# Gate of chunks 6 to 11 for two token blocks by seven half-depth products, with six weight decode steps at other places and the sums' lo parts on GpSimd

## The chip, the cores and the metric

The kernel runs on one core of a Trainium2 chip. The metric is the device time of one execution in microseconds. The profile's times are counted from the start of its span. PE is TensorE (matmul), PEld its weight loads, ACT is ScalarE, DVE is VectorE, POOL is GpSimd, SP is the engine whose queue issues most of the DMAs.

## What is computed

Attention over 2 batches of 8 heads (576 positions, depth 64, causal, with a bias from cumulative sums), and on its output x (1152 tokens of 512) two feed-forward layers:

```
xn = x / sqrt(mean(x*x) + 1e-6) * rms_g
g  = xn @ w_gate                    # 512 -> 1536
x  = (silu(g) * (xn @ w_val)) @ w_out
h  = x @ w_in                       # 512 -> 2048
out = (h * tanh(softplus(h))) @ w_out2
```

All of it is float32. The change is in the first layer's gate.

## The kernel before, in words

**Numbers.** A float32 matrix is held as two parts, hi (rounded to PE's format) and lo (what is left), and a product is three matmul passes: hi by hi, hi by lo, lo by hi (`PASS`). Weights arrive as 64-bit words and are decoded on the chip, 128x512 a unit. A unit's decode has these steps: `w_load` (L311 on, issue at L315) brings 512 KB into one of four buffers r0 to r3; `shift` (L326) and the Prelu of `w_a` (L337) on ACT prepare the lower and the upper word; `w_b` (L344) ORs them on DVE; `w_hi` (L351) casts the hi part on ACT; `w_c` (L360) subtracts on DVE for the lo part. One call of `w_tick` moves this line on by one unit, in the order of the list `seq`: it finishes unit n, ORs up to unit n+1 and prepares up to n+2, and issues each load whose buffer is free. If the place of the unit is not free yet (`free`), the tick does nothing.

**Order.** There is no planner in this part: the program text is the order of each engine's queue, and an engine works through its queue in order. Where a tick stands in the text decides what ACT and DVE have in front of the next operation that PE waits for.

**First layer.** The 1152 tokens are three blocks of 384 (0, 1, 2), the 1536 columns are 12 chunks f of 128. Unit 2f is the gate of chunk f, 2f+1 its value; they lie in a ring of eight places. `gate_val(b, f)` (matmuls at L672) makes both for one block, 24 matmuls into a bank pair of the pool psS (two such buffers); `silu` applies Silu on ACT and multiplies on DVE. Chunks are taken in pairs f, f+1 (f = 2, 4, 6, 8, 10). Block 0 is done by `gate_val`. For blocks 1 and 2 the gates are done by `gates` (L690, two calls of 24 matmuls, one Silu of 768 columns each), and the values by `vals`, a Strassen-like scheme over (two halves of depth) x (two chunks) x (two blocks): seven products of six matmuls (`product`, L714) in place of eight, in the order a, b, c, d, a, c, d, into four banks (three of psT, one of psX); three banks are used twice, and between the two uses ACT copies a to p (L775) and DVE adds b, c and d (`add`, L700).

**Sums.** Three of the seven products take sums of a pair's weights, which `s_pair` makes when the pair's second value unit is decoded: four DVE adds of 256 columns (L379), two hi casts on ACT (L382), two lo subtractions on DVE (L384). Until then the pair's decoded words stay in their r buffers, and no load can go there. The sums lie in places of the output weights' units 8 to 11. The sums of the inputs (`xt`) are made once, before the loop.

**The loop** (L1156 on) takes the pairs 4 to 10: for pairs above 4 two `plain` steps of block 0 (a `gate_val`, one or two ticks, a `silu`), two `gates` with a tick each, and `vals` with a tick behind its first d product (for pair 10 there two `h_split` instead, which split the first results for the output stage). Then comes the output stage `y_acc` (L817), which takes the four banks of psT and psX for block 0, and later the second layer (L841, L887).

Of the kernel before, what the change touches and what calls it, by code (L numbers as in the profile page):

```python
# [42 lines left out]
def tile_kernel(ctx: ExitStack, tc: tile.TileContext, kq, qq, v, s, w1, w2, rms_g, out):  # L43
# [145 lines left out]
    def gates(h, x, pools):  # L189
        co = slice(64 + 288 * x, 352 + 288 * x)  # L190
        t = []
        for y, (pool, tag) in enumerate(pools):
            t.append(pool.tile([128, 512], F32, tag=tag, name="gates"))
            nc.tensor.matmul(t[y][0:68, 0:288], sel[:, y, h], cC[0:48, 0, co], start=True, stop=True)
        nc.scalar.copy(out=KB[0][64:68, S * h + 288 * x:S * h + 288 * x + 288], in_=t[0][64:68, 0:288])

        for c, n, o in ((0, 288, 288 * x),) if h == 0 else (((0, 288, 704),), ((0, 224, 992), (224, 64, 640)))[x]:
            nc.scalar.copy(out=QB[0][64:68, o:o + n], in_=t[1][64:68, c:c + n])
# [26 lines left out]
    NI, NU1 = 2 * NF, 3 * NF  # L225
    NUW = NU1 + 2 * NF2

    VS = (2, 4, 6, 8, 10)
    FY = (10, 11) + tuple(range(10))

    def pair_units(j):

        return [2 * j, 2 * j + 1, 2 * j + 3, 2 * j + 2]

    seq = list(range(2 * NPRE)) + [NI] + pair_units(4) + pair_units(6) + [NI + 1, NI + 2]
    seq += pair_units(8) + [NI + 3, NI + 4] + pair_units(10) + [NI + n for n in (10, 11, 5, 6, 7, 8, 9)]
    seq += [NU1 + n for n in (0, 1, 2, 3, 4, 5, 6, 10, 12, 14, 7, 30, 31, 9, 11, 13, 8, 16, 18, 20, 22, 15, 24, 26, 17,
                              19, 28, 21, 23, 25, 27, 29)]
    wring = [sbt([128, 2, 512], F32R, f"ring{y}", f"wring{y}") for y in range(9)]
# [2 lines left out]
    def w14_unit(n):  # L242
        return w14[:, n // 3].rearrange("p (x a m) -> p x a m", x=3, a=2)[:, n % 3]
# [17 lines left out]
    def unit(n):  # L261

        if n < NI:
            return ring_unit(n % 8)
        if n < NU1:
            return w14_unit(n - NI)
        n -= NU1
        if n < 9:
            return ring_late((8, 3, 4, 5, 6, 7, 0, 1, 2)[n])
        if n < 15:  # L270
            return slot_unit((0, 11)[n % 2 == 0], (n - 9) // 2)
        if n < 27:
            return w14_unit((n - 5) % 12)
        return slot_unit((7, 5)[n // 3 - 9], n % 3)

    gv_done, y_done = set(), set()

    def free(n):

        if n < NI:  # L280
            return n < 8 or (NB - 1, n // 2 - 4) in gv_done
        if n < NU1:
            return len(gv_done) > 0 if n < NI + 8 else (NB - 1, 11 if n < NI + 10 else 9) in gv_done
        n -= NU1
        last = FY[-1]
        if n < 6 or n in (10, 12, 14):
            return (NB - 1, 9 if n == 1 else 11) in gv_done
        if n < 9:
            return (n - 6, 11) in y_done
        if n < 15:  # L290
            return (1, last) in y_done
        if n < 27:
            return (NB - 1, (n - 5) % 12) in y_done
        return ((NB - 1, 7) if n < 30 else (0, last)) in y_done
# [58 lines left out]
    def w_c(n, hi=True):  # L353
        if hi:
            w_hi(n)
        kept[n] = conv.pop(n)
        c = kept[n][:, :, 0].bitcast(F32)
        w = unit(seq[n])
        eng = nc.vector if mlp else nc.gpsimd
        eng.tensor_tensor(out=w[:, 1], in0=c, in1=w[:, 0].bitcast(F32), op=ALU.subtract)  # L360
        if val_of(seq[n]) is None:
            kept.pop(n)
        elif val_of(seq[n]):
            s_pair(seq[n] // 2 - 1, n)

    s_v = {}

    def s_area(f, a):

        return w14_unit(8 + 2 * (VS.index(f) % 2) + a).rearrange("p a m -> p (a m)")  # L370

    def s_pair(f, n):

        (l1, h1), (l2, h2) = ([r[:, :, x].bitcast(F32) for x in range(2)] for r in (kept.pop(n - 1), kept.pop(n)))
        lo, hi = slice(0, 256), slice(256, 512)
        for o, x, y, op in ((h2[:, hi], l2[:, lo], l2[:, hi], ALU.add), (h2[:, lo], l1[:, lo], l2[:, lo], ALU.subtract),
                            (h1[:, lo], h2[:, hi], l1[:, lo], ALU.subtract),
                            (h1[:, hi], l1[:, hi], h1[:, lo], ALU.subtract)):
            nc.vector.tensor_tensor(out=o, in0=x, in1=y, op=op)  # L379
        s_v[f] = h, l = [s_area(f, a) for a in range(2)]  # L380
        for o, x in ((512, h2), (0, h1)):
            nc.scalar.copy(out=h[:, o:o + 512], in_=x)  # L382
        for o, x in ((512, h2), (0, h1)):
            nc.vector.tensor_tensor(out=l[:, o:o + 512], in0=x, in1=h[:, o:o + 512].bitcast(F32), op=ALU.subtract)  # L384

    def val_of(n):

        f = n // 2
        return f % 2 if n < NI and n % 2 and f - f % 2 in VS[1:] else None

    def freed():

# [266 lines left out]
    def h_at(b, f, n=1):  # L659
        z, y = h_slot(b, f)  # L660
        return h_tile(z)[:, y] if n == 1 else h_tile(z)[:, y:y + n]
# [34 lines left out]
    def quarter(r, c, b):  # L696
        return xhl[r][:, 2 * c:2 * c + 2, TB * b:TB * b + TB]

    def add(o, x, y, op=ALU.add):
        nc.vector.tensor_tensor(out=o, in0=x, in1=y, op=op)  # L700
# [5 lines left out]
    def split_pair(h, l, src):  # L706
        nc.scalar.copy(out=h, in_=src)  # L707
        nc.vector.tensor_tensor(out=l, in0=src, in1=h.bitcast(F32), op=ALU.subtract)  # L708
# [41 lines left out]
    def val_restored():  # L750

        c = h_tile("w0")[:, 4:7].rearrange("p a n -> p (a n)")
        for x in range(2):
            w = unit(2 * (VS[0] + x) + 1).bitcast(F32)
            add(c[:, 512 * x:512 * x + 512], w[:, 0], w[:, 1])
        a11, a12, a21, a22 = (c[:, 256 * n:256 * n + 256] for n in range(4))
        for o, x, y, op in ((a22, a21, a22, ALU.add), (a21, a11, a21, ALU.subtract),
                            (a11, a22, a11, ALU.subtract), (a12, a12, a11, ALU.subtract)):
            add(o, x, y, op)
        s_v[VS[0]] = h, l = [s_area(VS[0], a) for a in range(2)]  # L760
        split_pair(h, l, c[:, 0:1024])

    def vals(f, gaps):


        w1_, w2_ = unit(2 * f + 1), unit(2 * f + 3)
        s2, s4, s3, s1 = ([t[:, 256 * n:256 * n + 256] for t in s_v[f]] for n in range(4))
        a11, a12, a22 = ([w[:, a, o:o + 256] for a in range(2)] for w, o in ((w1_, 0), (w1_, 256), (w2_, 256)))
        x = {(c, b): (quarter(0, c, b), quarter(1, c, b)) for c, b in ((0, 1), (1, 1), (1, 2))}
        h11, h12, h21, h22 = h_at(1, f), h_at(1, f + 1), h_at(2, f), h_at(2, f + 1)  # L770
        p, q = h_tile("w6")[:, 6], h_tile("w6")[:, 7]
        a, b, c = (psT.tile([128, 512], F32, tag="T", name=n)[:, 0:TB] for n in ("pa", "pb", "pc"))
        d = psX.tile([128, 512], F32, tag="X", name="pd")[:, 0:TB]
        product(a, a11, x[0, 1], True)
        nc.scalar.copy(out=p, in_=a)  # L775
        gaps[0]()
        product(b, s2, xt[2], True)
        add(p, p, b)
        product(c, s3, xt[3], True)
        add(q, p, c)  # L780
        product(d, s1, xt[1], True)
        add(q, q, d)
        gaps[1]()
        product(a, a12, x[1, 1], False)
        add(h22, h22, q, ALU.mult)
        add(h11, h11, a, ALU.mult)
        product(c, a22, xt[4], False)
        add(q, p, c)
        add(h12, h12, q, ALU.mult)
        product(d, s4, x[1, 2], False)  # L790
        add(p, p, d)
        add(h21, h21, p, ALU.mult)
        for z in (1, 2):
            gv_done.update(((z, f), (z, f + 1)))

    def h_split(b, f):
        h = h_at(b, f)
        h_t[b, f] = hhl = sbt([128, 2, TB], F32R, ("hA", "hB", "mm")[(NF * b + FY.index(f)) % 3], "hhl")
        nc.scalar.copy(out=hhl[:, 0], in_=h)  # L799
        nc.vector.tensor_tensor(out=hhl[:, 1], in0=h, in1=hhl[:, 0].bitcast(F32), op=ALU.subtract)  # L800
# [339 lines left out]
    def ticks(n):  # L1140
        def run():
            for _ in range(n):
                w_tick()
        return run

    def plain(b, f, n):
        gate_val(b, f)
        ticks(n)()
        silu(b, f)
# [3 lines left out]
    plain(0, 4, 1)  # L1153
    vals(VS[0], (nothing, ticks(1)))
    plain(0, 5, 1)
    for f in VS[1:]:  # L1156
        if f > 4:
            plain(0, f, 1)
            plain(0, f + 1, 2)
        gates(1, f, ticks(1))  # L1160
        gates(2, f, ticks(1))
        vals(f, (nothing, ticks(1)) if f < VS[-1] else (nothing, lambda: [h_split(*s) for s in steps2[:2]]))
    h_split(*steps2[2])
    for k, (b, f) in enumerate(steps2):
        if k:
# [117 lines left out]
```

## Time and profile before

| What | Value |
|---|---|
| median of 3 runs | 535.59 us (534.05 to 539.03) |
| the profiled execution's own time | 534.76 us |
| its span | 532.7 us |
| PE busy | 521.3 us, 2948 matmuls |
| DVE busy | 352.7 us |
| ACT busy | 309.9 us |
| POOL busy | 58.9 us, 72 instructions |

The profile is of one execution; the rows further down are from it. Neighbouring instructions of an engine overlap, so the step from one start to the next is a little shorter than the duration. POOL's last instruction in it starts at 112.84 us; the pairs 2 to 10 of the first layer lie between 150 and 262 us.

### The profile page before, as it was taken

The numbers are of one execution on the slowest core, as the hardware profiler recorded it, in microseconds if no ns is written. First come the engines' busy times: TensorE is split into PE (matmuls) and PEld (weight loads), VectorE is DVE, ScalarE is ACT, GpSimd is POOL, SyncE is SP. The second block draws the span as 40 slices with busy tenths as digits, with TensorE's granted clock in tenths as the row PEclk, the third lists the DMA queues.
The fourth block names the chain that finished last, engine by engine and source line by source line (L and its number), as shares of the span: only waits on it lengthen the run. The fifth ranks groups of instructions, "written<-read, shape, count | busy, mean of one in ns | idle before, by whom it ended". The sixth has DMA issues, their size and how long they took to land.

```text
span 532.7 us, 7987 instructions
## 1 busy us (share of the span) xinstructions
PE 521.3 (98%) x2948; PEld 471.6 (89%) x2948; DVE 352.7 (66%) x727; ACT 309.9 (58%) x664; POOL 58.9 (11%) x72
## 2 busy tenths in 40 slices
PE   7998999999999999999999999999999999999997
PEld 4776776689999999999999999999889999999885
DVE  7798999954878576675567666376578667653321
ACT  5687897876365565657378776586624433333211
POOL 6254666310000000000000000000000000000000
PEclk8699999999999999999999999999999999999999
DMA  9999797203013243535155635254101000000101
GB/s 222 264 194 279 208 249 173 81 19 140 1 41 119 78 144 136 157 119 159 40 159 162 180 96 156 80 158 140 60 0 49 11 1 0 2 0 1 59 1 59
DMA packets 18782, 55.90 MB, mean 105 GB/s; under 512 B 2348, under 2 KB 2604, under 8 KB 18716
## 3 DMA queue, kind: packets, MB, share of 16 engines
q1 hardware_dynamic: 13520, 42.04, 25.3%
q0 software_dynamic: 3712, 9.70, 8.9%
q10 hardware_dynamic: 1512, 3.66, 2.8%
q8 instruction: 23, 0.38, 0.3%
q14 instruction: 15, 0.12, 0.1%
HBM read 52.73 MB, written 2.66 MB: 104 GB/s over the span
## 4 chain that ended last, share of the span: by engine, by line
PE 91%; DVE 4%; ACT 2%; issue 1%; DMA 0%; ACTq 0%; DVEq 0%
PE o L887 12%; PE gv L672 12%; PE y L817 9%; PE gv L841 8%; PE gv L690 8%; PE gv L887 6%; PE pa L714 5%; PE pd L714 5%; PE pc L714 5%; PE gv L817 5%; PE xa L552 4%; PE tp L514 4%; PE pb L714 2%; PE sc L466 2%; PE sc L467 2%; ACT px L498 1%
## 5 line engine op out<-in xcount | busy, mean ns | idle before, releaser
L672 PE MATMUL gv<-xh,wring 128*128 128x384 f32 x256 | 67.1, 338 | 0.2 <-DVE h_w L681 0.2
L344 DVE SCALAR_TENSOR_TENSOR r<-r 128x512 int32<-128x512 int32 x68 | 47.5, 703 | 10.0 <-ACT r L337 7.1
L817 PE MATMUL y<-hhl,w 128*128 128x384 f32 x288 | 50.2, 334 | 0.0
L817 PEld LDWEIGHTS y<-hhl,w 128*128 128x128 f32 x288 | 49.9, 188 | 0.0
L672 PEld LDWEIGHTS gv<-xh,wring 128*128 128x128 f32 x256 | 46.4, 188 | 0.4 <-DVE h_w L681 0.3
L326 ACT ACTIVATE r<-r 128x512 int32<-128x512 uint8 x60 | 41.1, 686 | 7.1 <-DMA r<-in_w_dram 7.1
L498 ACT ACTIVATE px<-sc,cst 128x384 f32<-128x384 f32 (+2 forms) x80 | 41.2, 528 | 6.4 <-DVE cst L491 6.3
L672 PE MATMUL gv<-xl,wring 128*128 128x384 f32 x128 | 43.1, 336 | 0.0
L690 PE MATMUL gv<-xh,wring 128*128 128x384 f32 x160 | 41.6, 336 | 0.0
L491 DVE CUSTOM_DVE_ANT_0 sc<-sc,xtm 128x384 f32<-128x384 f32 (+4 forms) x72 | 34.6, 500 | 5.8 <-PE sc L467 3.0
L337 ACT ACTIVATE r<-r 128x512 f32<-128x512 f32 x57 | 38.3, 672 | 0.0
L514 PE MATMUL tp<-cst,px 128*128 128x128 f32 (+1 forms) x200 | 31.0, 286 | 2.1 <-DVE xl L631 1.4
L708 DVE TENSOR_TENSOR glb<-u,glb 128x768 fp32r<-128x768 f32 x20 | 19.1, 956 | 18.2 <-ACT glb L707 18.2
L514 PEld LDWEIGHTS tp<-cst,px 128*128 128x128 f32 (+1 forms) x200 | 24.1, 145 | 6.9 <-DVE xl L631 1.9
L552 PE MATMUL xa<-aw,px 128*64 128x320 f32 (+3 forms) x192 | 30.1, 380 | 0.0
L690 PEld LDWEIGHTS gv<-xh,wring 128*128 128x128 f32 x160 | 29.0, 188 | 0.0
L800 DVE TENSOR_TENSOR hhl<-h_w,hhl 128x384 fp32r<-128x384 f32 x30 | 16.6, 558 | 18.5 <-ACT hhl L799 18.5
L690 PE MATMUL gv<-xl,wring 128*128 128x384 f32 x80 | 26.9, 336 | 0.0
L887 PE MATMUL o<-wt,glb 128*128 128x512 f32 x108 | 26.9, 390 | 0.0
L887 PE MATMUL o<-w,glb 128*128 128x512 f32 x108 | 26.5, 390 | 0.0
L466 PE MATMUL sc<-w 128*128 128x384 f32 (+1 forms) x64 | 24.3, 390 | 1.6 <-POOL w L130 1.5
L817 PE MATMUL gv<-hhl,w 128*128 128x384 f32 x144 | 25.1, 334 | 0.0
(269 smaller groups left out, 1252.3 us busy)
## 6 DMA issues: line engine op xcount, KB each, us to landing
r<-in_w_dram SPq DMA_DIRECT2D x66, 512.0 KB, 4.0
w<-in_kq_dram POOLq DMA_DIRECT2D x7, 576.0 KB, 6.2
w<-in_qq_dram POOLq DMA_DIRECT2D x7, 576.0 KB, 6.9
out_dram<-osb SPq DMA_DIRECT2D x8, 256.0 KB, 2.1
px<-in_v_dram SPq DMA_DIRECT2D x5, 320.0 KB
r<-in_w_dram ACTq DMA_DIRECT2D x2, 512.0 KB, 4.5
px<-in_v_dram ACTq DMA_DIRECT2D x3, 320.0 KB
raw_hA<-in_kq_dram SPq DMA_DIRECT2D x3, 288.0 KB
```

The costliest lines, as they stand in the source:

```text
L326: nc.scalar.activation(out=low, in_=low.bitcast(U8)[:, :, 3], func=ACTF.Copy, scale=1 / 32, bias=-15.5 / 32)
L337: nc.scalar.activation(out=top, in_=top, func=ACTF.Prelu, scale=2.0 ** -112, alpha=-2.0 ** 32)
L344: nc.vector.scalar_tensor_tensor(out=low, in0=top, scalar=3, in1=low, op0=ALU.logical_shift_left, op1=ALU.bitwise_or)
L498: nc.scalar.activation(out=pv, in_=sv, func=ACTF.Exp, bias=sbias[:, c + x:c + x + 1], scale=-1.0, accum_out=ssum[:, sc:sc + 1])
L514: nc.tensor.transpose(t[0:rows, o - a:o - a + 128], P[pos[i] % 2][:, o:min(e, o + 128)], ident)
L552: nc.tensor.matmul(o, V[z][0:rows, c, ds], r, start=(c == 0), stop=(c == (1, 4)[part]))
L672: nc.tensor.matmul(t[:, g, 0:TB], w[:, a, 128 * c:128 * c + 128], xhl[r][:, c, TB * b:TB * b + TB], start=(n == 0), stop=(n == 11))
L690: nc.tensor.matmul(t[:, g, 0:TB], w[:, a, 128 * c:128 * c + 128], xhl[r][:, c, TB * b:TB * b + TB], start=(n == 0), stop=(n == 11))
L714: nc.tensor.matmul(t, A[a][:, 128 * c:128 * c + 128], B[r][:, c], start=(start and n == 0), stop=(n == 5), skip_group_check=True)
L817: nc.tensor.matmul(y_t[b][d], w[:, a, 128 * d:128 * d + 128], hhl[:, r], start=(f == FY[0] and y == 0), stop=(f == FY[-1] and y == 2))
L841: nc.tensor.matmul(t[:, x, 0:TB], w[:, a, 128 * c:128 * c + 128], xhl[r][:, c, TB * b:TB * b + TB], start=(n == 0), stop=(n == 11))
L887: nc.tensor.matmul(o_t[b][tt], gl[:, r, x, 128 * tt:128 * tt + 128], w[:, a], start=(g == 0 and x == 0 and y == 0), stop=(g == NG - 1 and ...
```

## The change

A new function `gate_set(f, beside)` computes the gates of the pair f for blocks 1 and 2 as `vals` computes the values: seven products in the order a, b, c, d, a, c, d, in the same four banks, with a copy on ACT, five adds on DVE and four Silus of 384 columns. It is used for the pairs 6, 8 and 10 (`GS`); the pairs 2 and 4 keep `gates`. Its weights' sums are made by `s_pair` from the two gate units, which are therefore kept as the value units are; they lie in the places of the output units 6 and 7. The order of units is changed so that each pair's units that are kept stand together. The ticks stand at other places: one within `gate_set` behind the first product, one in `vals` behind the first product and one behind the d product, one behind `vals`; one instead of two in the second `plain`. In pair 10 the tick behind d comes after the two `h_split`. The lo parts of all sums that `s_pair` makes (of values too) are subtracted on GpSimd.

```diff
-    VS = (2, 4, 6, 8, 10)
+    VS, GS = (2, 4, 6, 8, 10), (6, 8, 10)
...
-        return [2 * j, 2 * j + 1, 2 * j + 3, 2 * j + 2]
+        v, g = [2 * j + 1, 2 * j + 3], [2 * j, 2 * j + 2]
+        return v + g if j in GS else g[:1] + v + g[1:]
-    seq = list(range(2 * NPRE)) + [NI] + pair_units(4) + pair_units(6) + [NI + 1, NI + 2]
-    seq += pair_units(8) + [NI + 3, NI + 4] + pair_units(10) + [NI + n for n in (10, 11, 5, 6, 7, 8, 9)]
+    seq = list(range(2 * NPRE)) + [NI] + pair_units(4) + pair_units(6)
+    for j, n in ((8, 1), (10, 3)):
+        seq += [NI + n] + pair_units(j) + [NI + n + 1]
+    seq += [NI + n for n in (10, 11, 5, 6, 7, 8, 9)]
...
         if n < NI:
+            if val_of(n) and n % 2 == 0 and n // 2 - 1 > GS[0] and (1, n // 2 - 3) not in g_done:
+                return False
             return n < 8 or (NB - 1, n // 2 - 4) in gv_done
+        if n in (NI + 6, NI + 7):
+            return (1, GS[-1]) in g_done
...
-        s_v[f] = h, l = [s_area(f, a) for a in range(2)]
+        (s_v if val else s_g)[f] = h, l = [s_area(f, a, val) for a in range(2)]
         for o, x in ((512, h2), (0, h1)):
             nc.scalar.copy(out=h[:, o:o + 512], in_=x)
         for o, x in ((512, h2), (0, h1)):
-            nc.vector.tensor_tensor(out=l[:, o:o + 512], in0=x, in1=h[:, o:o + 512].bitcast(F32), op=ALU.subtract)
+            nc.gpsimd.tensor_tensor(out=l[:, o:o + 512], in0=x, in1=h[:, o:o + 512].bitcast(F32), op=ALU.subtract)
 
     def val_of(n):
         f = n // 2
-        return f % 2 if n < NI and n % 2 and f - f % 2 in VS[1:] else None
+        return f % 2 if n < NI and f - f % 2 in (VS[1:] if n % 2 else GS) else None
...
+    def gate_set(f, beside):
...
+        h11, h12, p, q = h_at(1, f), h_at(1, f + 1), h_at(2, f), h_at(2, f + 1)
+        a, b, c = (psT.tile([128, 512], F32, tag="T", name=n)[:, 0:TB] for n in ("ga", "gb", "gc"))
+        d = psX.tile([128, 512], F32, tag="X", name="gd")[:, 0:TB]
+        product(a, a11, x[0, 1], True)
+        nc.scalar.copy(out=p, in_=a)
+        beside()
+        product(b, s2, xt[2], True)
+        add(p, p, b)
+        product(c, s3, xt[3], True)
+        add(q, p, c)
+        product(d, s1, xt[1], True)
+        add(q, q, d)
+        nc.scalar.activation(out=q, in_=q, func=ACTF.Silu)
+        product(a, a12, x[1, 1], False)
+        nc.scalar.activation(out=h11, in_=a, func=ACTF.Silu)
+        product(c, a22, xt[4], False)
+        add(h12, p, c)
+        nc.scalar.activation(out=h12, in_=h12, func=ACTF.Silu)
+        product(d, s4, x[1, 2], False)
+        add(p, p, d)
+        nc.scalar.activation(out=p, in_=p, func=ACTF.Silu)
+        g_done.add((1, f))
...
+    def first():
+        h_split(*steps2[0])
+        h_split(*steps2[1])
+        w_tick()
+
     for f in VS[1:]:
+        last = f == VS[-1]
         if f > 4:
             plain(0, f, 1)
-            plain(0, f + 1, 2)
-        gates(1, f, ticks(1))
-        gates(2, f, ticks(1))
-        vals(f, (nothing, ticks(1)) if f < VS[-1] else (nothing, lambda: [h_split(*s) for s in steps2[:2]]))
+            plain(0, f + 1, 1 if f in GS else 2)
+        if f in GS:
+            gate_set(f, ticks(1))
+        else:
+            gates(1, f, ticks(1))
+            gates(2, f, ticks(1))
+        vals(f, (ticks(1) if f in GS else nothing, first if last else ticks(1)))
+        if f in GS and not last:
+            w_tick()
```

## Rows read from the trace of the kernel before

**Rows 1.** Busy us, share of the span and instructions by engine.
```profile
PE 521.3 (98%) x2948; PEld 471.6 (89%) x2948; DVE 352.7 (66%) x727; ACT 309.9 (58%) x664; POOL 58.9 (11%) x72
```

**Rows 2.** Busy time by stretch; last columns: granted clock, DMA share, GB/s.
```profile
50.00:100.00 50.00, 48.00 (x351) 34.92 (x349) 47.01 (x149) 44.07 (x147) 30.28 (x29) 1.00 0.77 199
...
150.00:200.00 50.00, 50.00 (x290) 50.00 (x289) 35.92 (x65) 28.31 (x48) 0.00 (x0) 1.00 0.30 93
200.00:250.00 50.00, 50.00 (x290) 50.00 (x289) 32.81 (x60) 30.25 (x52) 0.00 (x0) 1.00 0.44 139
250.00:300.00 50.00, 50.00 (x290) 50.00 (x290) 33.15 (x59) 35.16 (x67) 0.00 (x0) 1.00 0.45 132
```

**Rows 3.** The chain that ended last: start us, us, what (150 to 262 us).
```profile
158.71 4.16 PE gv L672 x24
...
222.35 8.32 PE gv L690 x48
230.67 1.04 PE pa L714 x6
...
236.95 1.07 PE pd L714 x6
...
262.00 24.96 PE y L817 x144
```

**Rows 4.** ACT's instructions in time order: start us, us, line, operation (pairs 6 and 8).
```profile
212.67 0.69 ACT L326 ACTIVATE r<-r 128x512 int32<-128x512 uint8 x1
213.24 0.67 ACT L337 ACTIVATE r<-r 128x512 f32<-128x512 f32 x1
213.80 0.66 ACT L326 ACTIVATE r<-r 128x512 int32<-128x512 uint8 x1
...
218.23 0.49 ACT L680 ACTIVATE h_w<-gv 128x384 f32<-128x384 f32 x1 [3.21 <-PE gv L672]
...
231.82 0.79 ACT L694 ACTIVATE h_w<-gv 128x768 f32<-128x768 f32 x1
232.51 0.46 ACT L775 COPY h_w<-pa 128x384 f32<-128x384 f32 x1
232.87 0.66 ACT L351 CAST wring<-r 128x512 fp32r<-128x512 f32 x1
```

**Rows 5.** DVE's instructions in time order (pair 6).
```profile
204.55 0.42 DVE L379 TENSOR_TENSOR r<-r 128x256 f32<-128x256 f32 x1
204.89 0.75 DVE L379 TENSOR_TENSOR r<-r,r 128x256 f32<-128x256 f32 x2
205.68 0.43 DVE L379 TENSOR_TENSOR r<-r 128x256 f32<-128x256 f32 x1
206.11 1.42 DVE L384 TENSOR_TENSOR w<-r,w 128x512 fp32r<-128x512 f32 x2
...
210.91 0.56 DVE L700 TENSOR_TENSOR h_w<-h_w,pd 128x384 f32<-128x384 f32 x1 [0.49 <-PE pd L714]
211.38 0.68 DVE L344 SCALAR_TENSOR_TENSOR r<-r 128x512 int32<-128x512 int32 x1
211.99 0.68 DVE L360 TENSOR_TENSOR wring<-r,wring 128x512 fp32r<-128x512 f32 x1
```

**Rows 6.** POOL by line and shape: count | busy us, mean ns | idle before.
```profile
L360 POOL TENSOR_TENSOR wring<-r,wring 128x512 fp32r<-128x512 f32 x8 | 10.4, 1298 | 21.0 <-ACT wring L351 15.1 <-issue 5.8
```

**Rows 7.** DVE's instructions in time order, 85 to 93 us.
```profile
85.96 0.73 DVE L491 CUSTOM_DVE_ANT_0 sc<-sc,xtm 128x512 f32<-128x512 f32 x1
...
87.46 1.71 DVE L344 SCALAR_TENSOR_TENSOR r<-r 128x512 int32<-128x512 int32 x1
```

**Rows 8.** POOL's instructions in time order, 85 to 93 us.
```profile
85.64 1.04 POOL L612 TENSOR_TENSOR w<-w,cst 128x512 f32<-128x512 f32 x1 [2.42 <-DVE cst L606]
...
87.11 1.50 POOL L136 TENSOR_TENSOR w<-raw_mm,w 64x576 fp32r<-64x576 f32 x1
```

**Rows 9.** Weight loads issued from 150 to 270 us: issue to landing.
```profile
DMA to landing us min/median/max: 3.5/3.6/4.6
```

More of the change, by code (lines that the diff above doesn't have):

```diff
@@ L274, in unit @@
         return slot_unit((7, 5)[n // 3 - 9], n % 3)
-    gv_done, y_done = set(), set()
+    gv_done, y_done, g_done = set(), set(), set()
     def free(n):
         if n < NI:
+            if val_of(n) and n % 2 == 0 and n // 2 - 1 > GS[0] and (1, n // 2 - 3) not in g_done:
+                return False
             return n < 8 or (NB - 1, n // 2 - 4) in gv_done
+        if n in (NI + 6, NI + 7):
+            return (1, GS[-1]) in g_done
         if n < NU1:
@@ L363, in w_c, with s_area, s_pair @@
         elif val_of(seq[n]):
[L364 to L372, printed above, removed]
+            s_pair(seq[n] // 2 - 1, n, seq[n] % 2)
+    s_v, s_g = {}, {}
+    def s_area(f, a, val=1):
+        return w14_unit(8 + 2 * (VS.index(f) % 2) + a if val else 6 + a).rearrange("p a m -> p (a m)")
+    def s_pair(f, n, val):
         (l1, h1), (l2, h2) = ([r[:, :, x].bitcast(F32) for x in range(2)] for r in (kept.pop(n - 1), kept.pop(n)))
@@ L761, in val_restored @@
         split_pair(h, l, c[:, 0:1024])
+    def gate_set(f, beside):
+        w1_, w2_ = unit(2 * f), unit(2 * f + 2)
+        s2, s4, s3, s1 = ([t[:, 256 * n:256 * n + 256] for t in s_g[f]] for n in range(4))
+        a11, a12, a22 = ([w[:, a, o:o + 256] for a in range(2)] for w, o in ((w1_, 0), (w1_, 256), (w2_, 256)))
+        x = {(c, b): (quarter(0, c, b), quarter(1, c, b)) for c, b in ((0, 1), (1, 1), (1, 2))}
+        h11, h12, p, q = h_at(1, f), h_at(1, f + 1), h_at(2, f), h_at(2, f + 1)
[20 more added lines that the diff above has]
+        g_done.add((1, f))
     def vals(f, gaps):
```

## The prediction

> **What bounds the kernel now.** I read the busy shares first, then the table by stretches, then the chain that ended last, and only then the queues of ScalarE (ACT) and VectorE (DVE) around one pair of chunks. The shares show a TensorE (PE) kernel with an idle GpSimd [rows 1]. The stretches show more: from 150 to 300 us PE is busy in all of every 50 us at clock 1.00, while DVE is busy in 33 to 36 and ACT in 28 to 35 of them [rows 2]. The chain is there one unbroken line of matmuls, in order of the code [rows 3]. So a matmul taken out between 150 and 300 us is won in full, and anything that makes PE wait there is lost in full. DVE and ACT have a third of their time free on average, but they work through their queues in order, so what decides is what stands in front of the one operation that PE waits for.
>
> **What is removed.** Gate chunks f, f+1 of blocks 1 and 2 now take 48 matmuls, 8.32 us; a product of six takes 1.04 us [rows 3]. Seven products take 7.28 us: 1.04 us less a pair, and three pairs (6, 8, 10) make **3.12 us**, 0.6%. The 48 matmuls wrote banks of their own and needed ACT only for one Silu pass at the end. The seven products go through four PSUM banks, three of them twice, and a bank's second product may start only when ACT or DVE has read the first: a's after the copy to p, c's after the second add, d's after the third. The same rule holds in the value set that follows, where today it costs nothing [rows 3].
>
> **What is added.** A pair's set adds a copy, five adds of 384 columns, and four activations of 384 columns in place of two of 768; its weights' sums add four DVE adds of 256 columns, two casts and two GpSimd subtractions; two DVE subtractions of 512 columns go from the value sums. On DVE that is 4 x 0.34 + 5 x 0.47 - 2 x 0.60 = 2.5 us more per pair by start-to-start times [rows 4, 5], of some 24 us, and about 2 us more on ACT. Both fit by the average. Where they stand is another matter.
>
> **Set of pair 6.** Time runs from the end of its first product a. ACT copies p (the next operation starts 0.36 later), and then comes the tick that the change puts right there: shift and top of gate chunk 9 (0.57 and 0.56), the hi cast of value chunk 9 (0.66) [rows 4]. DVE has done its two OR steps, waits for that cast, subtracts (0.60), makes the four sums of the value pair 8 (three starts 1.13 apart in all, and 0.34), and only then adds b to p (0.47) and c to p (0.55) [rows 5]. With about 0.03 for each change of engine: 0.03 + 0.36 + 0.57 + 0.56 + 0.66 + 0.03 + 0.60 + 1.47 + 0.47 + 0.55 + 0.03 = 5.3 us. PE wants bank c again after products b, c, d and a, 4 x 1.04 = 4.2 us. It waits **1.2 us**. Only time from rows at full length enters here, so I give it 1.0 to 1.4.
>
> **Set of pair 8.** Here a load is late as well. Time runs from the end of value set 6's first d product. DVE adds (0.47), subtracts for gate chunk 9 (0.60), makes two sums (0.77); ACT casts (0.66); GpSimd subtracts twice, at 1.30 each [rows 6], to 5.1 us. Only then are the two buffers free into which value chunks 10 and 11 are loaded; a load lands 3.5 to 4.6 us after its issue [rows 9], so at about 9.0 and 10.0. ACT prepares both (2 x 1.13, to 11.3), and behind them in its queue stand the Silu of gate (0,8) (0.49, to 11.8), the preparation of gate chunk 10, the hi cast, the Silu of (0,9) and the copy p. DVE goes on at 11.8 with the product for (0,8) (0.47) and two OR steps (1.2), waits for the cast until about 14.3, and has before the set's first two adds: two subtractions (1.2), the product for (0,9) (0.47), an OR step (0.6), four sums (1.47); then the adds (1.0). That ends at 19.1. PE has 3 products, 8.32 us of gates of block 0, one product and then the 4.2 us of cover: 16.6. It waits 2.5; without any delay of the loads beyond 3.5 us and with GpSimd undisturbed 1.8, with 4.6 us for both 2.9. I take **2.4 us**.
>
> **Set of pair 10** has the same late loads in front, but no sums in its tick: 1.47 less, **1.0 us** (0.4 to 1.5). **First output product:** in value set 10 DVE now has two splits (0.47, 0.55) and a tick (0.60, 0.60) between the third add (0.47) and the two products that free bank a (0.47, 0.55): 3.7 us against 3 products, 3.1 us of cover: **0.6 us** (0.3 to 0.8), which the ticks moved to the end cause.
>
> **What costs nothing.** The gate sums of pair 6 are made in value set 4 and used some 17 us later (two gates of 4.16 and the set's first products lie between), those of pairs 8 and 10 as far ahead: 3.5 us of casts and subtractions are hidden. The number of ticks until the output stage is the same, so the loads behind it stay as they were. The sums' area is that of output chunks 6 and 7, which are converted after the last set, before they are wanted. If that cover were gone, each would cost its cast and subtraction, 1.3 us a chunk [rows 4, 5].
>
> **GpSimd in place of DVE.** The two subtractions take 1.30 us each there, 0.69 on DVE [rows 5, 6], and they are not free of DVE: where a GpSimd operation on two SBUF inputs ran, a DVE step with two SBUF inputs took 1.71 us instead of 0.69 [rows 7, 8]; one with a PSUM input stayed at 0.73 [rows 7]. The set's adds read PSUM, so they pass; of the value set one product of two SBUF tiles meets the pair, about 1.2 us, between two idle gaps. The Trainium skill (GPSIMD Engine Reference, Engine selection) says to leave elementwise work on VectorE because GpSimd takes about twice as long on two inputs. The trace agrees on the ratio (1.9), but by the rule's choice the subtractions would stand on DVE ahead of the adds that PE waits for: some 1.4 us more at pairs 6 and 8, and the sum would come out about 3 us longer.
>
> **Sum.** 1.2 + 2.4 + 1.0 + 0.6 = 5.2 us of waits against 3.1 us of matmuls: **2.1 us longer**; with the low ends 3.5 - 3.1, 0.4 longer, with the high ends 6.6 - 3.1, 3.5 longer. The profiled execution took 534.76 us (span 532.7, the rest lies around it), the median of the runs shown is 535.59. From the middle of both, 535.2, I forecast **537.2 us**, in its own range 535.2 to 539.5. The waits of 1 to 2.5 us leave the clock alone, as from 50 to 100 us, where PE stood idle for 2.0 us and had 1.00 [rows 2].
>
> **Rivals.** *All is covered* (0.2): PE waits at none of the four places, the time falls by 3.1 us to 532.1. For it: DVE and ACT have 15 us and more of every 50 free [rows 2], and the same order of adds costs nothing in the value sets today [rows 3]. Against it: today no tick stands between the copy and the adds; in the changed set one does, with 3.2 us of DVE work.
>
> *GpSimd holds everything up* (0.15): its subtractions and DVE take turns, so that they last longer than the rows 6 say. A factor of 1.4 makes 1.8 us of 1.30; the loads come 1.0 us later, sets 8 and 10 wait 1.0 us more each, the copy p misses the second a product by another 0.3 in each, set 6 waits 0.3 more: about 3 us, 540.2 us. Below 1.5 us each it changes nothing that can be seen, from some 2.2 us on it makes the kernel slower by over 1%. For it: DVE's step of 1.71 us [rows 7]. Against it: all eight of this form have 1298 ns as their mean, with DVE busy beside them [rows 6]. The Trainium skill (SBUF — State Buffer, Who interferes with whom) says the port is locked for a whole instruction and the loser waits it out; the 1.71 us agree. By that rule alone the pair of subtractions would hold a two-input step for 2.6 us, which is inside this rival.
>
> *The sums come too late* (0.05): the set's second product waits for them. It would take more than 15 us of delay; a wait of 2 us a pair would make 539 us.
>
> **How the numbers follow.** Forecast 0.6, the rivals 0.2, 0.15 and 0.05. The range from 532.0 to 541.0 takes in the covered case and the GpSimd case. A measurement of this kernel (534.05 to 539.03 in three runs) tells about 1%, 5.4 us, from no change. Faster by over 1% would need 530.2, more than all that is removed: 0.03, for what the runs scatter. Slower by over 1% (541.0) is the far half of the GpSimd case and some of the sums': 0.09. Within 1%: 0.88.
>
> **What would show it.** In the profile after: 18 matmuls fewer; in the chain that ended last, PE waiting at the second c product of each set, released by DVE's add, for about 1.2, 2.4 and 1.0 us, and 0.6 before the first output product; GpSimd subtractions of 1.3 us, fourteen of them; ACT waiting for the loads of value chunks 10 and 11. If PE shows no idle time between 190 and 262 us, the covered case is right; if GpSimd's operations are near 2 us, the second rival is; if PE waits at a set's second product, the third.

## The result, and the profile after

The change makes the kernel **slower by 1.0%**: ratio 1.0097 to the kernel before, 95% interval 1.0069 to 1.0125. On 534.66 us, the median of before over 19 runs, that is 5.2 us, or 539.8 us; the forecast was 537.2, with a range from 532.0 to 541.0. The ratio leaves out three slow executions among the changed kernel's 19 (their median with these three is 541.61 us), and the profiled one, 545.65 us, is one of the three. Its attention, whose code is unchanged, ended 5.8 us later than in the trace before. So I compare one stretch from here on, from the first matmul of `gates` (pair 2) to the first of the second layer; the scatter of the attention's length lies ahead of it. Before it runs from 150.2 to 336.7 us, 186.5 us; after from 156.0 to 347.9 us, **191.9 us**. That is 5.4 us more and agrees with the ratio.

First the busy shares of the changed kernel, and the same table by stretches as [rows 2]:

```profile
PE 523.2 (96%) x2930; PEld 470.3 (86%) x2930; DVE 368.6 (68%) x746; ACT 315.9 (58%) x679; POOL 76.4 (14%) x86
```

```profile
150.00:200.00 50.00, 50.00 (x290) 50.00 (x289) 35.83 (x63) 28.79 (x48) 8.84 (x6) 1.00 0.21 65
200.00:250.00 50.00, 45.95 (x254) 45.32 (x253) 35.18 (x69) 30.96 (x57) 10.79 (x8) 0.97 0.32 115
250.00:300.00 50.00, 48.52 (x276) 47.56 (x275) 36.17 (x64) 36.04 (x69) 0.66 (x1) 1.00 0.51 158
...
235.00:240.00 5.00, 3.36 (x11) 3.36 (x12) 2.56 (x6) 3.62 (x7) 2.56 (x2) 0.70 0.16 29
240.00:245.00 5.00, 5.00 (x29) 5.00 (x29) 3.10 (x6) 2.04 (x4) 0.00 (x0) 0.96 0.45 180
```

There are 2930 matmuls, 18 fewer, and 14 more operations on GpSimd: the change does what it says. But PE, which was busy in all of each 50 us, now lacks 4.05 us between 200 and 250 and 1.48 between 250 and 300. And the clock, which had been 1.00, shows 0.97 in the second stretch; the drop lies between 235 and 245 us. Where PE waits is said by the table of waits (who waited for whom: us in total, times, longest):

```profile
PE gc L722 <- DVE h_w L708: 4.1, 2, 2.7
...
PE gc L722 <- DVE h_ring L708: 1.2, 1, 1.2
...
PE y L854 <- DVE h_w L708: 0.2, 1, 0.2
```

`gc` is the bank c of the sets, L708 is `add`: PE waits at the second c product of each of the three sets, and the table has no other wait in them. The set of pair 8 in PE's instructions in order of time (start us, us; between the lines stand further matmuls of the same product):

```profile
231.73 1.20 PE L722 MATMUL gd<-xt,w 128*128 128x384 f32 x6
232.77 0.34 PE L722 MATMUL ga<-xh,wring 128*128 128x384 f32 x1
...
236.64 0.44 PE L722 MATMUL gc<-xt_mm,wring 128*128 128x384 f32 x1 [2.67 <-DVE h_w L708]
238.45 0.52 PE L722 MATMUL gd<-xh,w 128*128 128x384 f32 x1
240.37 0.36 PE L722 MATMUL pa<-xh,wring 128*128 128x384 f32 x1
241.44 1.21 PE L722 MATMUL pb<-xt,w 128*128 128x384 f32 x6
```

From the second a to the second c it takes 3.87 us where 1.05 would do: a delay of 2.82. From there to `pa`, two products, it takes 3.73 us in place of the 2.21 that the other two sets need: another 1.5 us, in which the matmuls run at half the clock (0.50, the 1.2 GHz level, from 237 to 240 us). The same steps give 1.55 us for pair 6 (208.12 to 210.72) and 1.40 for pair 10 (260.23 to 262.68). The output stage's first products lose some 0.8 us: from the end of value set 10 to the second layer it takes 75.7 us, before 74.9.

How it comes to the 2.82 us is seen in ACT's and DVE's instructions in order of time, the queues that [rows 4, 5] show for the kernel before:

```profile
226.89 0.66 ACT L333 ACTIVATE r<-r 128x512 int32<-128x512 uint8 x1 [1.38 <-DMA r<-in_w_dram]
227.45 0.65 ACT L344 ACTIVATE r<-r 128x512 f32<-128x512 f32 x1
228.10 0.67 ACT L333 ACTIVATE r<-r 128x512 int32<-128x512 uint8 x1
228.67 0.64 ACT L344 ACTIVATE r<-r 128x512 f32<-128x512 f32 x1
229.21 0.48 ACT L688 ACTIVATE h_w<-gv 128x384 f32<-128x384 f32 x1
...
231.87 0.48 ACT L781 COPY h_w<-ga 128x384 f32<-128x384 f32 x1
```

```profile
229.72 0.56 DVE L689 TENSOR_TENSOR h_w<-h_w,gv 128x384 f32<-128x384 f32 x1 [3.48 <-ACT h_w L688]
...
233.31 0.68 DVE L367 TENSOR_TENSOR wring<-r,wring 128x512 fp32r<-128x512 f32 x1
233.92 0.42 DVE L387 TENSOR_TENSOR r<-r 128x256 f32<-128x256 f32 x1
234.25 0.75 DVE L387 TENSOR_TENSOR r<-r,r 128x256 f32<-128x256 f32 x2
235.04 0.43 DVE L387 TENSOR_TENSOR r<-r 128x256 f32<-128x256 f32 x1
235.38 0.55 DVE L708 TENSOR_TENSOR h_w<-h_w,gb 128x384 f32<-128x384 f32 x1
236.03 0.56 DVE L708 TENSOR_TENSOR h_w<-h_w,gc 128x384 f32<-128x384 f32 x1
```

The operation at the head of ACT's queue waits until 226.89 for the load of value chunk 10. The Silu of block 0 (L688), long ready, stands behind it and the three further steps that prepare the two units; DVE stands idle for 3.48 us for it. Then DVE works with only one gap of 0.15 us, but the four sums (L387) are ahead of the add of bank c.

A wait of ACT for a load is not new. In the kernel before, ACT waits as long in each of these pairs (1.79, 1.88 and 1.72 us; here pair 8), and PE waits nowhere:

```profile
225.30 0.67 ACT L326 ACTIVATE r<-r 128x512 int32<-128x512 uint8 x1 [1.88 <-DMA r<-in_w_dram]
```

There block 0's last Silu is done at 222.9, ahead of that wait, and the 8.3 us of `gates` give PE work meanwhile. So what stands behind the load should count, and not the wait alone; e2 and e8 test this.

### The profile page after: what moved, and what is told of

Its sections match the earlier page's. It is cut to its first block, busy times and chain, and to the rows that moved or that the text cites. A ratio compares the mean times of both kernels' runs of the same rounds, so it can differ in the third digit from the quotient of the medians.

```text
span 543.9 us, 8036 instructions
## 1 busy us (share of the span) xinstructions
PE 523.2 (96%) x2930; PEld 470.3 (86%) x2930; DVE 368.6 (68%) x746; ACT 315.9 (58%) x679; POOL 76.4 (14%) x86
## 4 chain that ended last, share of the span: by engine, by line
PE 60%; issue 17%; DVE 9%; ACT 6%; DMA 5%; POOL 2%; SPq 1%; POOLq 0%; ACTq 0%; DVEq 0%
PE o L924 12%; PE y L854 9%; PE gv L878 8%; PE gv L924 6%; PE gv L854 5%; DMA r<-in_w_dram 4%; PE xa L560 3%; PE pa L722 3%; PE pc L722 3%; PE pd L722 3%; PE tp L522 2%; POOL w L392 2%; DVE sc L499 2%; PE pb L722 2%; ACT px L506 1%
## 5 line engine op out<-in xcount | busy, mean ns | idle before, releaser
L680 PE MATMUL gv<-xh,wring 128*128 128x384 f32 x256 | 67.0, 338 | 0.2 <-DVE h_w L689 0.2
L351 DVE SCALAR_TENSOR_TENSOR r<-r 128x512 int32<-128x512 int32 x68 | 50.3, 748 | 4.5 <-ACT r L341 2.2
L680 PEld LDWEIGHTS gv<-xh,wring 128*128 128x128 f32 x256 | 46.4, 188 | 0.4 <-DVE h_w L689 0.3
L680 PE MATMUL gv<-xl,wring 128*128 128x384 f32 x128 | 43.0, 336 | 0.0
L522 PE MATMUL tp<-cst,px 128*128 128x128 f32 (+1 forms) x200 | 32.6, 293 | 6.2 <-DVE w L594 1.9
L392 POOL TENSOR_TENSOR w<-r,w 128x512 fp32r<-128x512 f32 x14 | 20.3, 1470 | 110.5 <-ACT w L390 93.2
L367 DVE TENSOR_TENSOR w<-r,w 128x512 fp32r<-128x512 f32 x24 | 16.4, 689 | 13.0 <-ACT w L358 12.4
L854 PEld LDWEIGHTS gv<-hhl,w 128*128 128x128 f32 x144 | 25.0, 188 | 0.0
```

Source lines behind the costliest of these rows:

```text
L351: nc.vector.scalar_tensor_tensor(out=low, in0=top, scalar=3, in1=low, op0=ALU.logical_shift_left, op1=ALU.bitwise_or)
L522: nc.tensor.transpose(t[0:rows, o - a:o - a + 128], P[pos[i] % 2][:, o:min(e, o + 128)], ident)
L680: nc.tensor.matmul(t[:, g, 0:TB], w[:, a, 128 * c:128 * c + 128], xhl[r][:, c, TB * b:TB * b + TB], start=(n == 0), stop=(n == 11))
L854: nc.tensor.matmul(y_t[b][d], w[:, a, 128 * d:128 * d + 128], hhl[:, r], start=(f == FY[0] and y == 0), stop=(f == FY[-1] and y == 2))
```

## The experiments

All ratios are to the kernel before, measured together with it on the same chip. The stretch is the one defined above, from one profile of each kernel; it is the difference of the two columns as shown, so its last digit can be off by 0.1. The two kernels in which PE waits nowhere in this stretch and does the same work, before and e7, differ by 0.3 us.

| Kernel | First gate product, us | Second layer, us | Stretch | Ratio (95%) |
|---|---|---|---|---|
| before | 150.2 | 336.7 | 186.5 | |
| after | 156.0 | 347.9 | 191.9 | 1.0097 (1.0069 to 1.0125) |
| e1, sums later | 151.7 | 340.8 | 189.1 | 1.0039 (1.0007 to 1.0072) |
| e2, prepared later | 151.2 | 339.2 | 188.0 | 1.0018 (0.9988 to 1.0048) |
| e3, lo parts on DVE | 151.3 | 349.0 | 197.7 | 1.0227 (1.0166 to 1.0287) |
| e4, fill | 154.6 | 346.4 | 191.8 | 1.0131 (1.0071 to 1.0191) |
| e5, three repairs | 151.0 | 336.1 | 185.1 | 0.9960 (0.9927 to 0.9992) |
| e6, gates as before | 154.1 | 345.2 | 191.1 | 1.0092 (1.0061 to 1.0123) |
| e7, GpSimd alone | 149.2 | 336.0 | 186.8 | 1.0000 (0.9968 to 1.0032) |
| e8, e6 prepared later | 147.7 | 335.6 | 187.9 | 1.0010 (0.9979 to 1.0041) |
| e9, e5 with DVE | 149.4 | 336.1 | 186.7 | 1.0003 (0.9971 to 1.0036) |

**e1, the value sums behind the second a product.** In `w_c` a pair's sums are put aside while the set's tick runs; no load may take their buffers meanwhile.

```diff
+            if hold:
+                pend.append((seq[n] // 2 - 1, n, seq[n] % 2))
+            else:
+                s_pair(seq[n] // 2 - 1, n, seq[n] % 2)
...
         nc.scalar.activation(out=h11, in_=a, func=ACTF.Silu)
+        sums_now()
         product(c, a22, xt[4], False)
```

> The tick inside the set no longer makes the value sums at once: their four adds, casts and GpSimd subtractions stand behind the second a product. Theory (DVE's queue in front of the set's adds is what PE waits for): the wait before the second c product, 1.55 / 2.82 / 1.40 us in the sets of pairs 6 / 8 / 10 of the profile after, becomes 0 / 1.5 / 1.5, as the four sums take 1.4 us and the tick of pair 10 has none; with it the stretch at clock 0.50 goes. Ratio to before 1.001 to 1.004. Rival (GpSimd's subtractions hold DVE and the loads): they are as many and as long, the waits keep their sum of over 5 us, ratio 1.008 or more.

Measured by the same steps as above: set 6 waits 0.1 us, set 8 1.7, set 10 1.7, and in sets 8 and 10 the second a product waits for ACT's copy p as well (0.2 and 0.7). The clock stays at 1.00 from 225 to 260 us. The stretch is 2.8 us shorter than after; 1.0039 is at the theory's upper end. The sums in DVE's queue are nearly the whole of set 6's wait. Set 10 waits more than after (2.4 in place of 1.4), which the theory did not have: with the copy p behind it, ACT waits until 250.10 for a further load, 2.3 us after the set's first product began; after, ACT could read this load at most 1.1 us after it. Why it is later here is not shown.

**e2, three ticks between load and preparation in pairs 8 and 10.**

```diff
-    AGE = 2
+    AGE = [2]
...
-            if m > n and done["t"] - loaded[m] < AGE:
+            if m > n and done["t"] - loaded[m] < AGE[0]:
...
+        AGE[0] = 3 if f in (6, 8) else 2
```

> From pair 8's steps to the end of pair 10 a unit is prepared on ACT one tick later after its load (3 ticks in place of 2); nothing else. Theory (ACT stands at the head of its queue waiting for late loads, and the Silu of block 0 and the copy p stand behind it): set 6 keeps its wait of 1.5 us, set 8 falls from 2.8 to about 0.3, set 10 from 1.4 to 0; no clock loss; ratio 0.998 to 1.002. Rival (only the DVE work of the tick counts): the same DVE work stands there, waits stay 2.8 and 1.4, ratio 1.008 or more.

Set 6 keeps 1.56 us (203.37 to 205.98), set 8 falls to 1.0 (expected 0.3), set 10 to 0.15, and the clock stays at 1.00. The stretch is 3.9 us shorter than after, though not an operation less is done. ACT still waits for the load of pair 8, but block 0's Silu now stands ahead of it (ACT in order of time):

```profile
220.67 0.49 ACT L688 ACTIVATE h_w<-gv 128x384 f32<-128x384 f32 x1
222.38 0.67 ACT L333 ACTIVATE r<-r 128x512 int32<-128x512 uint8 x1 [1.22 <-DMA r<-in_w_dram]
```

So the larger part of the loss is not work, and not the wait for the load as such, but what stands behind that wait in ACT's queue. What is left in set 8 is the sums ahead of the adds, as in set 6.

**e3, the lo parts of the sums back on DVE.** `nc.gpsimd` becomes `nc.vector` in `s_pair`.

> Only the sums' lo parts go back from GpSimd to DVE. Theory: DVE's queue gets two subtractions more in front of the adds (1.2 to 1.4 us) at sets 6 and 8: waits about 2.9, 4.4 and 1.6 us, 3 us more than the changed kernel, and two stretches of lost clock instead of one; ratio 1.014 to 1.022. Rival (GpSimd in place of DVE is what costs): loads are free 1.4 us earlier and nothing blocks, waits shrink, ratio 1.006 or less.

Sets 6, 8 and 10 wait 2.95, 4.6 and 1.5 us, and the clock falls twice (the table by stretches of this kernel):

```profile
205.00:210.00 5.00, 2.25 (x7) 2.25 (x8) 3.10 (x6) 1.67 (x4) 0.00 (x0) 0.76 0.45 142
...
235.00:240.00 5.00, 2.98 (x9) 2.98 (x10) 2.90 (x6) 2.21 (x6) 0.00 (x0) 0.50 0.62 206
```

The theory's waits and its two drops of the clock are there, and the rival falls. The ratio, of four runs, is 1.0227, at the top of the expected range (1.014 to 1.022). The subtractions on GpSimd save this change 5.8 us of stretch: the three waits add up to 9.1 us here and 5.8 after, and the two drops of the clock cost 3.3 us or more (from the second c to `pa` 3.69 and 4.01 us in place of 2.21), the one drop after 1.5.

**e4, matmuls in the time in which PE waits.** 7, 14 and 6 matmuls into a bank that nobody reads, between the second a and the second c product.

> Between the second a and the second c product of each set PE does 7, 14 and 6 matmuls more (1.2, 2.4 and 1.0 us) into a bank that nobody reads: work is added in time in which PE waits, so that it is not idle. Theory (the wait of 2.8 us in set 8 costs twice: in the profile after the granted clock is 0.50 for 3.3 us behind it and the two products there take 1.8 and 1.9 us instead of 1.05): clock 1.00 through set 8, these products 1.05 each, 1.5 us less than the changed kernel; ratio 1.005 to 1.008. Rival (the two products are slow for another reason): they stay at 1.8 and 1.9, ratio 1.009 or more.

Set 8's second c starts 3.94 us after the second a, as before the filling, but the clock stays at 1.00, and from there to `pa` it takes 2.21 us (PE in order of time):

```profile
235.63 0.44 PE L722 MATMUL gc<-xt_mm,wring 128*128 128x384 f32 x1 [0.30 <-DVE h_w L708]
...
237.84 0.34 PE L722 MATMUL pa<-xh,wring 128*128 128x384 f32 x1
```

So the 1.5 us are the clock's, as the theory had it. The time as a whole was a miss: the stretch stays at 191.8. From the set's first product to `pa`, set 10 takes 9.88 us here and 8.86 after; it gives back 1.0 of the 1.5 us, in waits for ACT's copy (0.55) and DVE's add. ACT waits there 1.16 us more for a load. It goes out 2.9 us ahead of the set's first product in both kernels (250.60 here, 253.15 after), but ACT can read it only 5.2 us after its issue here, and within 4.0 after. With one profile of each kernel it stays open whether that is chance. The ratio of 1.0131 (four runs) is wide and does not decide between theory and rival: its interval holds the theory's upper end and most of the rival's range. The clock and the length of the two products do.

**e6, the gates computed as before, all else as in the change.** It leaves out the use of the gate sums, which are still made.

```diff
-            gate_set(f, ticks(1))
+            gates(1, f, ticks(1))
+            gates(2, f, nothing)
+            g_done.add((1, f))
```

> The changed kernel's order, ticks, gate sums and GpSimd subtractions, but the gates of pairs 6 to 10 computed by two calls of 24 matmuls as before (the sums of the gates are made and not used). Theory (PE waits because a set's banks are used twice with DVE's queue between): no wait in the gates although all the other work is there; only the output stage's first product waits 0.3 to 0.7 us; stretch 186.8 to 187.6, ratio 1.000 to 1.003. Rival (the added work as such delays the chain, wherever the products stand): PE waits in vals or for weights, stretch 189 or more, ratio 1.006 or more.

This is a miss, and the most useful one. PE does wait, at another place, in pairs 8 and 10 (1.69 and 1.64 us). First PE of this kernel in order of time, then ACT, then DVE:

```profile
225.87 0.34 PE L680 MATMUL gv<-xh,wring 128*128 128x384 f32 x1
227.89 0.44 PE L698 MATMUL gv<-xh,wring 128*128 128x384 f32 x1 [1.69 <-DVE h_w L689]
```

```profile
224.50 0.67 ACT L333 ACTIVATE r<-r 128x512 int32<-128x512 uint8 x1 [1.53 <-DMA r<-in_w_dram]
...
226.78 0.47 ACT L688 ACTIVATE h_w<-gv 128x384 f32<-128x384 f32 x1
```

```profile
227.28 0.55 DVE L689 TENSOR_TENSOR h_w<-h_w,gv 128x384 f32<-128x384 f32 x1 [3.58 <-ACT h_w L688]
```

`gates` needs a bank pair of psS, and block 0's Silu and product, which would free it, stand behind the load. So the seven products are not needed for this wait: when block 0's Silu is late, PE meets it at whatever wants its bank. In pair 6 ACT waits 1.19 us for a load too (until 200.54), but block 0's first Silu stands ahead of it (198.29), and PE waits nowhere.

**e8, e6 with e2's edit.**

> The kernel of e6 (48 matmuls a pair as before, the change's order, ticks, gate sums and GpSimd) with one edit, that of e2: in pairs 8 and 10 a unit is prepared three ticks after its load. New theory (e6's waits of about 2 us at the gates of pairs 8 and 10 are the late loads: ACT stands at its queue's head for them, block 0's Silu stands behind, and with it the bank pair that the gates want): both waits go, only the output stage's first products wait (0.9 us), stretch from the first gate product to the second layer 187.0 to 188.0 instead of 191.1; ratio 1.000 to 1.004. Rival (the sums' and subtractions' mere work delays DVE): the same work is there, waits stay, stretch over 190, ratio 1.007 or more.

Both waits are gone, and the stretch is within the expected one. Of its 1.4 us more than before, 1.0 lie in the output stage, and 0.5 are small delays, of 0.1 us each, ahead of the second c and d products of value sets 8 and 10. So 3.2 us of e6's loss come from block 0's Silu standing behind the late loads, and the added sums and subtractions as such cost at most the 0.5 us.

**e7, GpSimd alone**, that is, the kernel before with the lo parts of its value sums on GpSimd.

> The kernel before with one edit: the lo parts of the value sums on GpSimd. Theory: two operations of 1.3 us each a pair, off the path; DVE is relieved of 1.2 us a pair that nobody waits for; stretch 186.5 within 0.3, ratio 0.998 to 1.002. Rival (GpSimd and DVE taking turns at SBUF holds the chain up): waits before the value sets' products, stretch over 187.5, ratio over 1.004.

As the theory said: PE waits nowhere, 186.8 us. By itself the edit is neither gain nor loss that can be seen (0.3 us of stretch, interval of the ratio 0.9968 to 1.0032).

**e5, three repairs together**: e1's and e2's edits, and the tick of `first` behind the value set.

```diff
         h_split(*steps2[1])
-        w_tick()
...
-        if f in GS and not last:
+        if f in GS:
             w_tick()
```

> The changed kernel with the value sums behind the second a product, with three ticks between load and preparation in pairs 8 and 10, and with the last tick of value set 10 behind the set instead of ahead of the products that free bank a. Theory: each of the three takes away one group of waits (set 6 and half of set 8; the rest of set 8 and set 10; the output stage's first product), so PE waits nowhere from 200 to 270 us for more than 0.3 us and the 18 matmuls are won: the stretch from the first gate product to the second layer, 186.5 us before and 191.9 after, becomes 183.4 to 184.5; ratio 0.993 to 0.998. Rival (what is added costs engines that matter elsewhere, GpSimd's subtractions or block 0's Silus among them): new waits take the old ones' place, stretch over 186.5, ratio 1.000 or more.

The stretch is 185.1 us, 1.4 shorter than before and 0.6 above what was expected; the ratio 0.9960 lies below 1 with its whole interval. Of the 3.1 us that the 18 matmuls are worth, 1.7 still go: the waits of the weight loads ahead of matmuls (PEld) in this kernel add up to that.

```profile
PEld pc L733 <- DVE h_w L719: 0.7, 2, 0.5
PEld y L868 <- DVE h_w L719: 0.4, 1, 0.4
PEld gc L733 <- DVE h_ring L719: 0.3, 1, 0.3
PEld gc L733 <- DVE h_w L719: 0.3, 1, 0.3
```

**e9, e5 with the lo parts on DVE.**

> The kernel of e5 with the sums' lo parts back on DVE. Theory (DVE's queue decides, GpSimd's subtractions cost nothing where they are): DVE has 1.2 us more at each of the sums, which stand behind the second a product now and delay the sets' last adds and the value sets' first ones; waits of 0.5 to 1.5 us come back at pairs 6 and 8, stretch 186 to 188.5 instead of 185.1, ratio 0.999 to 1.007. Rival (GpSimd blocks DVE as long as it relieves it): stretch 185.1 within 0.5, ratio 0.996.

1.6 us more than e5, with 1.7 us of PE waiting in the value sets' c products. The theory holds. Against e3 the price of DVE has shrunk from 5.8 us to 1.6: the subtractions are dear where they stand ahead of what PE wants.

## Why the prediction was right, and where it was off

**Right: the direction and its mechanism.** The matmuls went (18, 3.1 us), and PE lost more than that at exactly the four places named, released by DVE's add or, in the output stage, by DVE as well. e1, e2 and e3 take away, take away and add the parts of the chain that the prediction built, and the waits follow, but for set 10 in e1. Measured, 539.8 us lies in the range and 2.6 us above the forecast, just beyond its own range of 535.2 to 539.5 (its low and high sums give 535.6 to 538.7).

**Off by size: the waits.** 1.2, 2.4, 1.0 and 0.6 us were forecast, 1.55, 2.82, 1.40 and 0.8 were found: 6.6 in all in place of 5.2 (6.6 is also the sum of the prediction's high ends). Three terms were mis-sized. The set's adds depend on each other, and the step from one to the next is 0.65 us (235.38 to 236.03), not the 0.47 taken from neighbours that do not. The cover was counted from the start of product b, the chain from the end of product a: the copy p starts 0.20 us after b (204.98 to 205.18), so that four products cover 4.0 us and not 4.2. These two are the 0.35 us by which set 6 was short. And GpSimd's two subtractions took 3.2 us in the value sets 6 and 8 instead of 2.6, as DVE's products of two SBUF tiles meet them (one such product takes 1.10 us at 222.50, and 0.55 at 219.85); in the gate sets, where DVE's adds read PSUM, the pair kept 2.6:

```profile
220.03 3.16 POOL L392 TENSOR_TENSOR w<-r,w 128x512 fp32r<-128x512 f32 x2 [7.82 <-PE pc L722]
235.49 2.56 POOL L392 TENSOR_TENSOR w<-r,w 128x512 fp32r<-128x512 f32 x2 [12.30 <-ACT w L390]
...
L392 POOL TENSOR_TENSOR w<-r,w 128x512 fp32r<-128x512 f32 x14 | 20.3, 1470 | 110.5 <-ACT w L390 93.2 <-PE pc L722 17.3
```

The mean is 1470 ns for 1298 in [rows 6], a factor of 1.13. The second rival put 1.8 us each and said that below 1.5 nothing would be seen; the pairs in the value sets, at 1.6 each, lie between. The loads behind it went out at 223.2 us, 5.9 us after the product from which the prediction counted 5.1. In the figure for set 8 this hardly shows, and that is luck: the prediction lets DVE wait for the hi cast until 14.3 us after that product, and it is 14.4, although all in front of it is 0.6 us later. The cast needs only the first of the two OR steps (230.20 and 0.69 long, the cast at 230.92); the prediction had it about 0.6 us too late, as if it stood behind the second, and the two misses cancel.

**Wrong: "the waits leave the clock alone".** They did not: set 8 lost 1.5 us to clock 0.50. The stretch from 50 to 100 us, on which that step rested, has its 2.0 us of idle time in three pieces, the longest 0.98 us; here 2.67 us were in one piece. In e4, with the full clock at set 8, set 10 waited 1.0 us longer; whether the drop's share of the total is therefore smaller than 1.5 us, one profile of each does not show. Added up for the profile: 6.6 + 1.5 - 3.1 = 5.0 us of the 5.4 found. The rest is nearly all in the two products behind each second c, which take 2.21 us in place of 2.09, three times.

**The rivals.** All covered: no, at none of the places. GpSimd holds everything up: its 540.2 us is nearer to the measured 539.8 than the forecast is, but the copy p, which it has miss the second a product, misses none after (a follows d by 1.04 us in each set, 231.73 to 232.77 in pair 8's), and e7 and e3 speak against it; its part is the 0.6 us by which the loads are later. Sums too late for their set: no run shows PE waiting at a set's second product (its price, put at 539 us, comes to 538.1 by the prediction's own figures: 535.2 - 3.1 + 3 x 2). The Trainium skill's rule that elementwise work belongs on VectorE (GPSIMD Engine Reference, Engine selection) was weighed with 3 us for this kernel. e3 makes this choice and is 5.8 us longer than the change: the 3 us are there in the waits (9.1 in place of 5.8), and the second drop of the clock, which the prediction did not have, is most of the rest.

**What the prediction did not separate.** It put the late loads down to set 8 and 10 as a term in a chain. e2 and e8 show that the order around them is a cause of its own: the new order keeps four units a pair in the four load buffers, so the next pair's loads start only when its sums are through, and two ticks later ACT waits for them with block 0's Silu behind. Of the 5.4 us lost, e2 gets back 3.9 and e1 2.8 (the 1.5 us of the clock are in both), together with the tick of e5 6.8.

## What to carry to other kernels

Here the place of an operation in its queue counted more than its cost: look for the one that PE waits for, and list what stands ahead of it, waits for loads included. When work is moved off PE, price the products removed against the bank's second use: seven products with banks used twice need their reader within four products, 4.0 us here. And when a buffer is kept longer, its next load lands later, so look what stands behind the instruction that first reads it, and move that instruction back.

## What the runs showed of the hardware that was not expected

- After single idle stretches of PE of 2.67 us (after), 2.80 and 4.35 us (e3) the matmuls that followed ran at granted clock 0.50, the 1.2 GHz level, and two products took 1.5 to 1.8 us longer; after waits of up to 1.69 us (e1, e2, e6, and sets 6 and 10 of after) the clock stayed at 1.00. With unused matmuls in the wait (e4) it stayed at 1.00 too.
- DVE's adds of 384 columns start 0.47 us apart when they are independent (219.85, 220.31, 220.78 in after) and 0.65 us apart when each adds a bank to what the one ahead wrote (235.38, 236.03).
- The same 512 KB load, ahead of set 10, could be read by ACT within 4.0 us of its issue in after and only 5.2 us after it in e4, which adds nothing but unused matmuls; set 10 waits 1.0 us longer there.
- The attention's end (the first gate product) scatters from 147.7 to 156.0 us over these eleven profiles with the same code ahead of it; a difference of 1% is not to be read from one execution's total.
